# Transposing q and k on VectorE instead of TensorE in a fused attention and Fourier-mixing kernel

## Chip, cores and metric

The kernel runs on one core of a Trainium2 chip. The metric is the device time of one launch in microseconds. Lower is better; what is given is the median of ten executions. The profile is of one execution of the ten.

## What is computed

The reference is an attention with a threshold, followed by a Fourier mixing layer with a two-layer network. Cut to what matters:

```python
# q, k, v: [batch 8, heads 8, seq 576, head_dim 64] float32; tau a scalar
scores = 0.125 * q @ k.T                         # per batch and head, 576 x 576
thresh = max(scores, -1) - tau
scores = where(scores >= thresh, scores, -1e9)
attn = exp(scores - max(scores, -1));  attn /= sum(attn, -1) + 1e-9
x = (attn @ v)  -> [8, 576, 8 * 64]              # heads side by side
mixed = real(fft(fft(x, axis=1), axis=2))
u = x + mixed
out = u + relu(layernorm(u) @ w_ch1) @ w_ch2     # 512 -> 2048 -> 512
```

All of it is in float32. The change touches only the way in which q and k reach the product of the scores.

## The kernel before

**Pairs and steps.** The eight heads of a batch are worked in four pairs, so there are 32 pairs, numbered n. Head 0 of a pair lies on partitions 0 to 63, head 1 on 64 to 127. The 576 queries of a pair are worked in five steps (t = 0 to 4): four of 128 queries, in which each head has its own score tile, and one of the last 64 queries, in which both heads share one tile (head 0's queries on its upper half, head 1's on its lower). The main loops run over i = 5 n + t.

**How q and k get transposed.** The score product contracts over head_dim, so q and k are needed with head_dim on the partitions: `qT` and `kT`, 128 x 576 each for the pair. `load_pair(n)` brings both heads' rows into one tile `qk` (nine blocks of 128 rows by 2 x 64 values, one buffer) with ten transfers. `prep_pair(n)`, or its generator `prep_in_parts(n)`, turns the nine blocks on TensorE, through three PSUM banks: `pq` (four blocks of q, L398), `pk` (four of k, L405) and `pt` (the last 64 rows of both, L409). VectorE empties `pq` into `qT` and multiplies by the scale on the way (L399), ScalarE empties `pk` into `kT` (L406), and VectorE empties the two halves of `pt` (L410, L413). Then the transfers of pair n + 1 are issued.

In `kT`, head 1's keys stand with its last 64 first, because of where the transfers put them; the later transposition of the weights relies on that order.

**Scores.** `scores(i)` multiplies, for t < 4, 64 rows of `qT` with halves of 288 keys of `kT`, one product per head and half (L433); the two heads' products use the two row halves of the array. For t = 4 there are five products of 64 x 64 weights (L444), head 1's cut into three because of the order of its keys. Each product in float32 is two instructions of TensorE.

**After the scores.** `softmax(i)` takes the maxima on VectorE (L461), the exponentials on ScalarE (L469), the threshold (L473), and the comparison with the sum on VectorE (L477). The score tiles (`sc`, two buffers, four PSUM banks) are free after that. One step later `weights_in_parts` transposes the weights on TensorE (`pe` L541 and L544, `pw` L560), ScalarE copies them out, and after steps 2 and 0 `weighted_values` multiplies them with v (L589). The four remaining PSUM banks (`mm`) are shared by everything else.

**The order of work.** In the first batch (`step`, pairs 0 to 3) and the second (`second_batch`, pairs 4 to 7) the program's order is each engine's order. During the first batch the weights are also read, converted (L288 to L320) and centred, and TensorE is kept busy with idle products (`busy`, L112). From the third batch on (the last loop, pairs 8 to 31) the program's order is kept for TensorE alone; the other engines' and the transfers' orders come from a planner. There `fill()` puts the mixing and the network of the earlier batches (L822, L848, L926, L1090) between the pieces of the attention, so many products to each step. When the attention is through, the rest of the network is worked off.

Before, the preparation of the next pair stands at the end of step 4 in the first batch, at step 3 of the second, and in three parts over step 3 in the last loop.

Of the kernel before, what the change touches and what calls it, by code (L numbers as in the profile page):

```python
# [47 lines left out]
def kernel(  # L48
# [75 lines left out]
    def load_pair(n, queue=nc.sync):  # L124
        b, p = n // NPAIR, PAIRS[n % NPAIR]
        hs = [2 * p + (j + p) % 2 for j in range(2)]

        qk = sb.tile([128, 9, 2, D], FP32, tag="qk", bufs=1, name="qk_in")
        for j, h in enumerate(hs):
            nc.sync.dma_start(  # L130
                out=qk[:, 0:4, j, :], in_=q[b, h, 0:512, :].rearrange("(t p) d -> p t d", p=128)
            )
            nc.sync.dma_start(out=qk[0:64, 8, j, :], in_=q[b, h, 512:576, :])


        h = hs[0]
        queue.dma_start(
            out=qk[:, 4:8, 0, :], in_=k[b, h, 0:512, :].rearrange("(t p) d -> p t d", p=128)
        )
        queue.dma_start(out=qk[64:128, 8, 0, :], in_=k[b, h, 512:576, :])  # L140
        h = hs[1]
        queue.dma_start(out=qk[0:64, 4, 1, :], in_=k[b, h, 512:576, :])
        rows = k[b, h, 0:512, :].rearrange("(t r p) d -> p r t d", r=2, p=64)
        queue.dma_start(out=qk[64:128, 4:8, 1, :], in_=rows[:, 0])
        queue.dma_start(out=qk[0:64, 5:8, 1, :], in_=rows[:, 1, 0:3])
        queue.dma_start(out=qk[64:128, 8, 1, :], in_=rows[:, 1, 3])
        loaded[n] = qk

    def load_v(n):

# [20 lines left out]
    for u in range(2):  # L171
        for j in range(2):
            nc.gpsimd.memset(v_in[u][64 - 64 * j : 128 - 64 * j, 8 + j, :], 0.0)
    eps = const.tile([128, 1], FP32, name="eps")
    nc.vector.memset(eps[:], 1e-6)

# [205 lines left out]
    xs = {}  # L382
    sums = {}

    def prep_pair(n):
        for _ in prep_in_parts(n):
            pass

    def prep_in_parts(n):


        qk = loaded.pop(n)
        qT = sb.tile([128, S], FP32, tag="qT", name="qT")
        kT = sb.tile([128, S], FP32, tag="kT", name="kT")

        pq = ps.tile([128, 512], FP32, tag="mm", bufs=4, name="pq")
        for t in range(4):
            nc.tensor.transpose(pq[:, 128 * t : 128 * t + 128], qk[:, t, :, :], ident[:, :])  # L398
        nc.vector.tensor_scalar(  # L399
            out=qT[:, 0:512], in0=pq[:, :], scalar1=q_scale[:, :], scalar2=None, op0=ALU.mult  # L400
        )
        yield
        pk = ps.tile([128, 512], FP32, tag="mm", bufs=4, name="pk")
        for t in range(4):
            nc.tensor.transpose(pk[:, 128 * t : 128 * t + 128], qk[:, 4 + t, :, :], ident[:, :])  # L405
        nc.scalar.copy(kT[:, 0:512], pk[:, :])  # L406
        yield
        pt = ps.tile([128, 512], FP32, tag="mm", bufs=4, name="pt")
        nc.tensor.transpose(pt[:, 0:128], qk[:, 8, :, :], ident[:, :])  # L409
        nc.vector.tensor_scalar(  # L410
            out=qT[:, 512:S], in0=pt[:, 0:64], scalar1=q_scale[:, :], scalar2=None, op0=ALU.mult
        )
        nc.vector.tensor_copy(kT[:, 512:S], pt[:, 64:128])  # L413
        heads[n] = (qT, kT, v_in[n % 2])
        if n + 1 < B * NPAIR:
            load_pair(n + 1)

    def normalized(n):

# [3 lines left out]
    def scores(i):  # L423
        n, t = divmod(i, NT)
        qT, kT = heads[n][0:2]

        nh = 2 if t < 4 else 1
        sc = [ps.tile([128, 2, 512], FP32, tag="sc", name=f"sc{j}") for j in range(nh)]
        if t < 4:
            for c in range(2):  # L430
                for j in range(2):
                    hp = slice(64 * j, 64 * j + 64)
                    nc.tensor.matmul(  # L433
                        sc[j][:, c, 0:HALF], qT[hp, 128 * t : 128 * t + 128],
                        kT[hp, HALF * c : HALF * (c + 1)], start=True, stop=True,
                    )
        else:

            for j, c, c0, k0, w in (
                (0, 0, 0, 0, HALF), (1, 0, 0, 64, HALF), (0, 1, 0, HALF, HALF),  # L440
                (1, 1, 0, 64 + HALF, 512 - HALF), (1, 1, 512 - HALF, 0, 64),
            ):
                hp = slice(64 * j, 64 * j + 64)
                nc.tensor.matmul(  # L444
                    sc[0][hp, c, c0 : c0 + w], qT[hp, 512:S], kT[hp, k0 : k0 + w],
                    start=True, stop=True, skip_group_check=True,
                )
        steps[i] = (sc, nh)

# [735 lines left out]
    def step(i):  # L1185

        n, t = divmod(i, NT)
        scores(i)

        def last_stages():  # L1190
            run = chunks.pop(i - 1, None)
            for _ in range(2 if run else 0):
                next(run, None)

        if t == 1 and n > 0:
            softmax(i, lambda: weighted_values(n - 1, 1), last_stages)
            load_v(n + 1)
        elif t == 3:
            softmax(i, lambda: weighted_values(n, 0), last_stages)
        else:  # L1200
            softmax(i, None, last_stages)
        if t == 1 and n > 0:
            pass
        elif later and later[0][0] <= i:
            later.pop(0)[1](i)
        else:
            busy(2 if i < NCHUNK else 1)
        if t == NT - 1:
            prep_pair(n + 1)
        if i in chunks:  # L1210
            next(chunks[i])
        if i > 0:
            transposed_weights(i - 1)
        if i in chunks:
            next(chunks[i])
        while after and after[0][0] <= i:
            after.pop(0)[1]()
        if i > 0 and i + 3 < NCHUNK:
            chunks[i + 3] = w1_chunk(i + 3)
        if t == 2 and n > 0:  # L1220
            folds.append(fold_rows(n - 1))
        if folds and next(folds[0], True):
            folds.pop(0)
# [27 lines left out]
    raw = load_dim()  # L1251
    load_seq()
    chunks[1] = w1_chunk(1)
    prep_pair(0)
    load_v(0)
    chunks[2] = w1_chunk(2)
# [59 lines left out]
    def second_batch(i):  # L1316

        nonlocal budget
        n, t = divmod(i, NT)
        first = i - per_batch  # L1320
        if first != 1:
            scores(i)
        if first == 0:

            transposed_weights(i - 1)
        softmax(i, None, lambda: (advance(first - 1), advance(first - 1)))
        chunks.pop(first - 1, None)
        transfers(first)
        fold_more()
        if first == 0:  # L1330
            weighted_values(n - 1, 1)
            scores(i + 1)
            column_means(LAST)
            copy_mean(LAST)
            folds.append(fold_rows(n - 1))
            while folds:
                fold_more()
            load_v(n + 1)
            start_batch(0)
            mix(3)  # L1340
            mix(3)
        elif first == 1:
            mix(3)
            transposed_weights(i - 1)
            mix(2)
            mirrored(LAST)
            for c, eng in ((1, nc.vector), (3, nc.vector), (0, nc.gpsimd), (2, nc.gpsimd)):
                less_mean(eng, LAST, c)
            advance(first)
            advance(first)  # L1350
        elif first == 2:
            mix(2)
            transposed_weights(i - 1)
            mix(2)
            weighted_values(n, 0)
            advance(first)
            advance(first)
        else:
            fill()
            transposed_weights(i - 1)  # L1360
            advance(first)
            advance(first)
            fill()
            if t == 3:
                prep_pair(n + 1)
            fill()
            if t == 2:
                weighted_values(n, 0)
            if t == 0:
                weighted_values(n - 1, 1)  # L1370
                folds.append(fold_rows(n - 1))
                load_v(n + 1)
        if first == 16:
            fold_halves(1)
        if first < 3:
            budget += 3 * per_slot
# [10 lines left out]
    for i in range(2 * per_batch, total + 1):  # L1387
# [4 lines left out]
        n, t = divmod(i, NT)  # L1392
        if t > 2:
            fold_more()
        nothing = iter(())
        prep = prep_in_parts(n + 1) if t == 3 and n + 1 < B * NPAIR else nothing
        weights = weights_in_parts(i - 1)
        next(prep, None)
        fill()
        next(weights, None)  # L1400
        fill()
        next(weights, None)
        next(prep, None)
        if i < total:
            softmax(i)
        fill()
        next(prep, None)
        if t == 2:
            weighted_values(n, 0)
        if t == 0:  # L1410
# [60 lines left out]
```

## Time and profile before

| what | value |
|---|---|
| median of 10 runs | 1669.63 us (1667.75 to 1671.06) |
| the profiled execution's own time | 1667.75 us |
| its span, first to last instruction | 1665.9 us |
| granted TensorE clock | 0.998 |
| packets of q1, the queue of SP's transfers | 128854, 55.35 MB, 12.3% of 16 engines |
| q transfers: 64 of 128 KB and 64 of 16 KB | 2.3 and 2.2 us to landing |
| k transfers on SP: 31 of 128, 31 of 64, 31 of 48 and 93 of 16 KB | 2.1 to 2.4 us to landing |

How to read it: the span is the time from the first instruction to the last as the profiler saw them; what lies around it (1.85 us here) belongs to the time too. PE is TensorE's matmul row, PEld its weight loads, DVE VectorE, ACT ScalarE, POOL GpSimd, SP the engine that issues most transfers. A PE that is busy all the time need not be at its peak, since matmuls are pipelined and their ends are modelled. In the groups of instructions, a row gives line, engine, operation, what is written and read, shapes and count, then busy time and the mean of one in ns, then the idle time of the engine just before and who ended it.

### The profile page before, as it was taken

Reading aid. Unit: us, or ns where it says so; the run is one execution under the profiler, and the core shown is the slowest. Engines: PE = TensorE matmul, PEld = TensorE weight load, DVE = VectorE, ACT = ScalarE, POOL = GpSimd, SP = SyncE. Lnnn points to the kernel's source line nnn. Section 1 sums busy time; section 2 is a strip of 40 time slices with the busy share of each in tenths; the row PEclk is TensorE's granted clock in tenths of the full one; section 3 lists DMA queues with packets and bytes.
Section 4 is the critical chain, followed back from the end, with each engine's and each line's share of the span. In section 5 each row is a group of like instructions: output and inputs, shape, how many; then the busy total and the mean of one; then the engine's idle time right before and its main releaser. Section 6 shows DMA issues by size and latency. Waiting matters only on the chain.

```text
span 1665.9 us, 28885 instructions
## 1 busy us (share of the span) xinstructions
PE 1616.9 (97%) x10826; PEld 1271.8 (76%) x10826; DVE 1146.1 (69%) x2518; ACT 838.0 (50%) x1817; POOL 583.5 (35%) x779
## 2 busy tenths in 40 slices
PE   8998999999999999999999999999999999999998
PEld 4555555577887778878888788887878787889998
DVE  6887785567757686857575868686777768664454
ACT  5765775444455454545354546454646455532111
POOL 5774562042311452133331143214242244115232
PEclk9999999999999999999999999999999999999999
DMA  5423221100010001010001010101001010000000
GB/s 165 114 55 110 73 87 43 34 15 22 22 35 19 24 15 42 23 28 14 23 22 35 15 28 15 43 22 29 22 17 41 22 32 4 14 1 13 14 13 13
DMA packets 130384, 57.48 MB, mean 35 GB/s; under 512 B 121123, under 2 KB 121125, under 8 KB 130246
## 3 DMA queue, kind: packets, MB, share of 16 engines
q1 hardware_dynamic: 128854, 55.35, 12.3%
q8 instruction: 86, 1.41, 0.3%
q14 instruction: 52, 0.43, 0.1%
q10 hardware_dynamic: 1392, 0.30, 0.1%
HBM read 46.02 MB, written 9.44 MB: 33 GB/s over the span
## 4 chain that ended last, share of the span: by engine, by line
PE 75%; DVE 14%; ACT 7%; issue 2%; POOL 1%; DMA 0%; SPq 0%; DVEq 0%; ACTq 0%; POOLq 0%
PE ph L926 23%; PE po L1090 18%; PE pv L589 8%; PE sc L433 7%; PE pw L560 5%; PE po L848 3%; DVE e L477 3%; DVE neg L461 2%; ACT e L469 2%; DVE hs L1051 2%; PE sc L444 2%; PE ph L822 1%; PE py L692 1%; PE pa L709 1%; PE pn L782 1%
## 5 line engine op out<-in xcount | busy, mean ns | idle before, releaser
L469 ACT ACTIVATE e<-sc,neg 128x576 f32<-128x576 f32 x288 | 212.5, 738 | 236.3 <-DVE neg L461 235.6
L461 DVE TENSOR_REDUCE neg<-sc 128x1 f32<-128x576 f32 x288 | 206.2, 751 | 170.9 <-PE sc L433 158.7
L477 DVE SCALAR_TENSOR_TENSOR e<-sc,thr,e 128x576 f32<-128x576 f32 x288 | 229.8, 811 | 57.5 <-ACT thr L473 54.1
L1090 PE MATMUL po<-w,hs 128*128 128x256 f32 x1024 | 246.3, 383 | 0.5 <-DVE u L804 0.5
L1090 PEld LDWEIGHTS po<-w,hs 128*128 128x128 f32 x1024 | 186.0, 190 | 33.6 <-issue 11.2
L926 PE MATMUL ph<-u_t,w 128*128 128x128 f32 x1536 | 187.2, 276 | 0.0
L926 PEld LDWEIGHTS ph<-u_t,w 128*128 128x128 f32 x1536 | 178.7, 192 | 4.4 <-issue 3.3
L560 PE MATMUL pw<-ident,e 128*128 128x128 f32 x1152 | 169.5, 274 | 10.4 <-ACT kT L406 2.7
L562 ACT COPY e_t<-pw 128x512 f32<-128x512 f32 x256 | 148.7, 595 | 59.8 <-PE pw L560 59.1
L433 PE MATMUL sc<-kT,qT 64*128 64x288 f32 x1024 | 168.0, 429 | 7.0 <-DVE e L477 6.4
L560 PEld LDWEIGHTS pw<-ident,e 128*128 128x128 f32 x1152 | 134.2, 141 | 29.3 <-issue 4.3
L935 DVE TENSOR_TENSOR hs<-ph,hs 128x512 f32<-128x512 f32 x160 | 107.0, 685 | 71.3 <-PE ph L926 46.7
L433 PEld LDWEIGHTS sc<-kT,qT 64*128 64x128 f32 x1024 | 92.9, 186 | 69.0 <-issue 37.2
L926 PE MATMUL ph<-t_u,s_w 128*128 128x128 f32 x1024 | 126.0, 276 | 2.2 <-POOL t_u L900 1.8
L804 DVE SCALAR_TENSOR_TENSOR u<-po,rstd,u 128x256 f32<-128x256 f32 (+1 forms) x164 | 75.5, 484 | 73.8 <-PE po L1090 71.9
L926 PEld LDWEIGHTS ph<-t_u,s_w 128*128 128x128 f32 x1024 | 119.4, 192 | 5.3 <-issue 2.6
L1090 PE MATMUL po<-hs,s_tile 128*128 128x256 f32 x512 | 122.0, 382 | 0.0
L496 ACT ACTIVATE e<-e,den 128x576 f32<-128x576 f32 x96 | 74.9, 780 | 67.3 <-DVE den L489 66.6
L1090 PEld LDWEIGHTS po<-hs,s_tile 128*128 128x128 f32 x512 | 93.6, 190 | 13.6 <-issue 2.1
L943 ACT ACTIVATE hs<-hs 128x512 f32<-128x512 f32 x112 | 69.3, 630 | 64.0 <-DVE hs L935 63.9
L622 POOL TENSOR_TENSOR half<-x 128x287 f32<-128x287 f32 x48 | 40.7, 869 | 126.1 <-ACT x L595 70.7
L1086 POOL TENSOR_TENSOR hs<-hs,s_tile 128x512 f32<-128x512 f32 x32 | 42.4, 1325 | 117.5 <-PE po L1090 113.8
(199 smaller groups left out, 2900.8 us busy)
## 6 DMA issues: line engine op xcount, KB each, us to landing
hs<-in_moe_w_ch_dram SPq DMA_DIRECT2D x23, 512.0 KB, 4.3
out_dram<-u SPq DMA_DIRECT2D x36, 256.0 KB, 2.2
qk_in<-in_q_dram SPq DMA_DIRECT2D x64, 128.0 KB, 2.3
v_in<-in_v_dram SPq DMA_DIRECT2D x64, 128.0 KB, 2.4
qk_in<-in_k_dram SPq DMA_DIRECT2D x31, 128.0 KB, 2.4
w<-in_moe_w_ch_dram SPq DMA_DIRECT2D x6, 512.0 KB, 7.6
qk_in<-in_k_dram SPq DMA_DIRECT2D x31, 64.0 KB, 2.3
stage<-in_moe_w_ch_dram SPq DMA_DIRECT2D x3, 512.0 KB, 3.8
```

Of the source, the lines that this page charges most:

```text
L433: nc.tensor.matmul(sc[j][:, c, 0:HALF], qT[hp, 128 * t : 128 * t + 128], kT[hp, HALF * c : HALF * (c + 1)], start=True, stop=True,)
L461: nc.vector.tensor_reduce(out=neg[:, j : j + 1], in_=sc[j][:, :, 0:HALF], axis=AXIS_XY, op=ALU.max, negate=True,)
L469: nc.scalar.activation(out=ej, in_=sc[j][:, :, 0:HALF], func=ACT.Exp, bias=neg[:, j : j + 1], scale=1.0)
L477: nc.vector.scalar_tensor_tensor(out=ej, in0=sc[j][:, :, 0:HALF], scalar=thr[:, j : j + 1], in1=ej, op0=ALU.is_ge, op1=ALU.mult, accum_out ...
L496: nc.scalar.activation(out=e[:, S : 2 * S], in_=e[:, S : 2 * S], func=ACT.Copy, scale=den[:, 1:2])
L560: nc.tensor.transpose(pw[:, c, :], e[:, c0 : c0 + 128], ident[:, :])
L562: nc.scalar.copy(e_t[:, 4 * j : 4 * j + 4, qs], pw[:, :, :])
L589: nc.tensor.matmul(pv[64 * j : 64 * j + 64, 0:m], vt[:, 2 * c + j, :], e_t[:, 4 * j + c, 0:m] if c < 4 else ends[:, 0:m], start=(c == 0), ...
L804: nc.vector.scalar_tensor_tensor(out=u, in0=product, scalar=self.rstd[:, t : t + 1], in1=u, op0=ALU.mult, op1=ALU.add,)
L926: nc.tensor.matmul(banks[name][:, 128 * q : 128 * q + 128], left[c][:, 512 * part + 128 * q : 512 * part + 128 * q + 128], right[c], start ...
L935: nc.vector.tensor_tensor(out=to, in0=bank, in1=to if other is None else other, op=ALU.add)
L1090: nc.tensor.matmul(bank[:, 0 : DM // 2], left[p], right[p], start=start and p == 0, stop=p == NK - 1, skip_group_check=True,)
```

## The change

`load_pair` now fills two tiles, `q_in` and `k_in` (128 x 576, one buffer each), with eight transfers. Each takes 32 of the 64 columns of one head, all 576 rows, and places every block of 32 rows side by side on 32 partitions, in runs of 128 bytes. VectorE then transposes each 32 x 32 block where it stands (`nc.vector.transpose`), and the result is head_dim by position.

`prep_pair` has three such transpositions: k's 576 columns, once more the last 64 keys of head 1 into the columns ahead of them (so that head 1's keys can still be read with the last 64 first; `kT` is 64 columns wider), and q's 576 columns into `qT`, which has one buffer now instead of two. TensorE's nine transpositions, the PSUM banks and the four copies out of them are gone.

The scaling of q is an operation of its own, `scale_q`: on ScalarE for pair 0, else on GpSimd, in place, at step 2 of the pair before. `prep_ends`, at step 1, copies the two heads' last 64 queries on GpSimd into a 128 x 128 tile `q_ends` that is zero elsewhere; the scores of step 4 are then two products of 128 x 128 weights with both heads' keys.

The preparation of the next pair stands at step 3 everywhere, in one piece: in the first batch and the second behind the softmax of that step, in the last loop ahead of it in the program.

```diff
 def load_pair(n, queue=nc.sync):
-        qk = sb.tile([128, 9, 2, D], FP32, tag="qk", bufs=1, name="qk_in")
...
+        raws = []
+        for src, name, eng in ((q, "q_in", nc.sync), (k, "k_in", queue)):
+            raw = sb.tile([128, S], FP32, tag=name, bufs=1, name=name)
+            for j, h in enumerate(hs):
+                for g in range(2):
+                    p = 64 * j + 32 * g
+                    eng.dma_start(
+                        out=raw[p : p + 32, :].rearrange("p (r d) -> p r d", d=32),
+                        in_=src[b, h, :, 32 * g : 32 * g + 32].rearrange(
+                            "(r p) d -> p r d", p=32
+                        ),
+                    )
+            raws.append(raw)
+        loaded[n] = raws
...
+    q_ends = const.tile([128, 128], FP32, name="q_ends")
+    nc.gpsimd.memset(q_ends[:, :], 0.0)
...
+    def scale_q(n):
+        raw = loaded[n][0]
+        if n == 0:
+            nc.scalar.activation(out=raw[:, :], in_=raw[:, :], func=ACT.Copy, scale=q_scale[:, :])
+        else:
+            nc.gpsimd.tensor_scalar(
+                out=raw[:, :], in0=raw[:, :], scalar1=q_scale[:, :], scalar2=None, op0=ALU.mult
+            )
...
 def prep_pair(n):
...
+        q_raw, k_raw = loaded.pop(n)
+        kT = sb.tile([128, D + S], FP32, tag="kT", name="kT")
+        nc.vector.transpose(kT[:, D : D + S], k_raw[:, :])
+        nc.vector.transpose(kT[64:128, 0:D], k_raw[64:128, 512:S])
+        qT = sb.tile([128, S], FP32, tag="qT", bufs=1, name="qT")
+        nc.vector.transpose(qT[:, :], q_raw[:, :])
...
+    def prep_ends(n):
+        for j in range(2):
+            hp = slice(64 * j, 64 * j + 64)
+            nc.gpsimd.tensor_copy(q_ends[hp, hp], heads[n][0][hp, 512:S])
...
 def scores(i):
...
-                    hp = slice(64 * j, 64 * j + 64)
+                    hp, k0 = slice(64 * j, 64 * j + 64), D * (1 - j)
...
-                        kT[hp, HALF * c : HALF * (c + 1)], start=True, stop=True,
+                        kT[hp, k0 + HALF * c : k0 + HALF * (c + 1)], start=True, stop=True,
...
-            for j, c, c0, k0, w in (
-                (0, 0, 0, 0, HALF), (1, 0, 0, 64, HALF), (0, 1, 0, HALF, HALF),
-                (1, 1, 0, 64 + HALF, 512 - HALF), (1, 1, 512 - HALF, 0, 64),
-            ):
-                hp = slice(64 * j, 64 * j + 64)
+            for c in range(2):
                 nc.tensor.matmul(
-                    sc[0][hp, c, c0 : c0 + w], qT[hp, 512:S], kT[hp, k0 : k0 + w],
-                    start=True, stop=True, skip_group_check=True,
+                    sc[0][:, c, 0:HALF], q_ends[:, :], kT[:, D + HALF * c : D + HALF * (c + 1)],
+                    start=True, stop=True,
                 )
...
-        if t == NT - 1:
+        if t == 2:
+            scale_q(n + 1)
+        if t == 3:
             prep_pair(n + 1)
+        if t == 1:
+            prep_ends(n)
```

The last lines are of the first batch (`step`); the second batch and the last loop get the same three calls. At the start, `scale_q(0)` stands ahead of `prep_pair(0)`.

More of the change, by code (lines that the diff above doesn't have):

```diff
@@ L126, in load_pair @@
         hs = [2 * p + (j + p) % 2 for j in range(2)]
-        qk = sb.tile([128, 9, 2, D], FP32, tag="qk", bufs=1, name="qk_in")
[L129 to L147, printed above, removed]
+        raws = []
[12 more added lines that the diff above has]
+        loaded[n] = raws
     def load_v(n):
@@ L383 @@
     sums = {}
-    def prep_pair(n):
[L386 to L413, printed above, removed]
+    def scale_q(n):
[6 more added lines that the diff above has]
+            )
+    def prep_pair(n):
+        q_raw, k_raw = loaded.pop(n)
[4 more added lines that the diff above has]
+        nc.vector.transpose(qT[:, :], q_raw[:, :])
         heads[n] = (qT, kT, v_in[n % 2])
@@ L1253 @@
     chunks[1] = w1_chunk(1)
+    scale_q(0)
     prep_pair(0)
@@ L1372, in second_batch @@
                 load_v(n + 1)
+        if t == 1:
+            prep_ends(n)
+        if t == 2:
+            scale_q(n + 1)
         if first == 16:
@@ L1394 @@
             fold_more()
-        nothing = iter(())
-        prep = prep_in_parts(n + 1) if t == 3 and n + 1 < B * NPAIR else nothing
         weights = weights_in_parts(i - 1)
-        next(prep, None)
+        if t == 1:
+            prep_ends(n)
+        if t == 2 and n + 1 < B * NPAIR:
+            scale_q(n + 1)
+        if t == 3 and n + 1 < B * NPAIR:
+            prep_pair(n + 1)
         fill()
@@ L1402 @@
         next(weights, None)
-        next(prep, None)
         if i < total:
@@ L1406 @@
         fill()
-        next(prep, None)
         if t == 2:
```

## The prediction

> **What bounds the kernel now.** I read the page from the top: busy time by engine, then the slices, then the same by stage (the windows view), and last the order of instructions around one preparation of a pair.
>
> ```profile
> PE 1616.9 (97%) x10826; PEld 1271.8 (76%) x10826; DVE 1146.1 (69%) x2518; ACT 838.0 (50%) x1817; POOL 583.5 (35%) x779
> ...
> PE   8998999999999999999999999999999999999998
> PEld 4555555577887778878888788887878787889998
> DVE  6887785567757686857575868686777768664454
> ```
>
> PE is full nearly everywhere, but PEld is not: in slices 1 to 6 weight loads are at 5 tenths while VectorE is at 7 to 8. There the PE row is filled by `busy` (L112), which computes nothing. The windows (after the two times: PE, PEld, DVE, ACT, POOL busy, clock, DMA share, GB/s) split the kernel:
>
> ```profile
> 66.00:105.00 39.00, 36.22 (x199) 21.30 (x197) 33.94 (x76) 30.62 (x71) 30.32 (x32) 1.00 0.34 92
> ...
> 282.00:1480.00 1198.00, 1181.22 (x8243) 952.74 (x8242) 835.45 (x1858) 617.31 (x1317) 354.92 (x473) 1.00 0.09 24
> ```
>
> In the first batch VectorE is busy 33.9 of 39 us, in a loop scores, maximum, exponent, threshold. From 282 us, where the third batch begins, to 1480 us TensorE is idle 1198.0 - 1181.2 = 16.8 us for 24 pairs, 49 us each (some 9.8 us for each of five steps). There a microsecond taken off TensorE is nearly a microsecond of the kernel, if nobody else falls behind. TensorE's timeline of one pair in that stage shows what the change touches (start, duration, instruction, idle before it):
>
> ```profile
> 1036.99 1.24 PE L433 MATMUL sc<-kT,qT 64*128 64x288 f32 x8
> 1038.16 0.66 PE L398 MATMUL pq<-ident,qk_in 128*128 128x128 f32 x4
> 1038.78 1.99 PE L1090 MATMUL po<-w,hs 128*128 128x256 f32 x8
> ...
> 1041.37 0.66 PE L560 MATMUL pw<-ident,e 128*128 128x128 f32 x4 [0.48 <-DVE qT L399]
> ...
> 1044.03 0.60 PE L405 MATMUL pk<-ident,qk_in 128*128 128x128 f32 x4
> 1044.47 2.76 PE L1090 MATMUL po<-hs,s_tile 128*128 128x256 f32 x12
> 1047.06 0.27 PE L409 MATMUL pt<-ident,qk_in 128*128 128x128 f32 x1
> 1047.26 1.20 PE L444 MATMUL sc<-kT,qT 64*64 64x288 f32 x10
> 1048.39 0.92 PE L1090 MATMUL po<-hs,s_tile 128*128 128x256 f32 x3
> ```
>
> Durations overlap, so I read start to next start: pq 0.62, pk 0.44, pt 0.20, the last 64 queries' scores 1.13 us. Once, pw waited 0.48 us because the pq bank was still being emptied by VectorE.
>
> **What the skill says.** "VectorE: DVE Perf Modes", The three transpose paths: VectorE transposes 32x32 blocks only, into SBUF; so the blocks must be placed by the transfer, as the diff does. No row of this trace is such a transposition. "Vector Engine (DVE) Microarchitecture Reference", The reshape front-end: the transposition sustains one element per cycle per lane. "SBUF — State Buffer", SBUF: two separate sides: VectorE and GpSimd exclude each other on a shared port pair; the trace agrees, `e<-e,den` (L492) takes 0.52 us alone and 1.54 us at 1035.80, beside a 1.93 us GpSimd operation. "DMA: Bandwidth & Descriptors", Why small descriptors are slow: at 256 bytes and below each packet's fixed cost tells; here q1's 128854 packets took 12.3% of 16 x 1665.9 us, 25.4 ns each at 430 bytes on average.
>
> **TensorE, 24 late pairs.** 23 preparations lose nine transpositions. By the gaps above they are 0.62 + 0.44 + 0.20 = 1.26 us; at the steady pace (pk: four in 0.44) 9 x 0.11 = 0.99. I take 1.1: 25.3 us. The last scores go from ten instructions on quarters of the array, two running side by side, to four full ones (two products, two passes each). Eight 256-column instructions follow each other at 0.216 us in the chain of waits (1.73 us), so 288 columns are 0.243 and four are 0.97: a gain of only 1.13 - 0.97 = 0.16 us, 24 times, 3.8 us. The waits of pw on qT, 1.9 us in this stage, go too. Sum 31.0 us.
>
> **VectorE.** Three evictions go, two transpositions of 576 and one of 64 columns come.
>
> ```profile
> L399 DVE TENSOR_SCALAR qT<-pq,q_scale 128x512 f32<-128x512 f32 x32 | 23.7, 739 | 5.3 <-PE pq L398 5.3
> L410 DVE TENSOR_SCALAR qT<-pt,q_scale 128x64 f32<-128x64 f32 x32 | 8.8, 276 | 6.8 <-PE pt L409 6.8
> L413 DVE COPY kT<-pt 128x64 f32<-128x64 f32 x32 | 6.8, 213 | 0.0
> ```
>
> Removed: 0.74 + 0.28 + 0.21 = 1.23 us a pair. Added: by the Perf Modes page (58 cycles + one per element at 0.96 GHz) 0.66 us for 576 columns, an estimate; the bounds are L492's 0.52 and two cycles per element, about 1.3 us. I take 0.68 twice and 0.15, 1.51 us: net +0.3 a pair, from 0 to +1.6. Late in the kernel VectorE has 1198 - 835 = 363 us to spare, 15 us a pair, which hides it on average. But all 1.5 us now stand in one place, ahead of the maxima of step 3 (t = 3), and the qT transposition waits there for that step's scores, since qT has one buffer. Queued behind it: maximum, threshold, then TensorE's next scores, which need the `sc` buffers. At 1036.99 VectorE was itself 1.1 us late with the maxima, and freed `sc` at 1042.7, 4.5 us ahead of the next scores. 1.5 us fits. I give back 4 us for the pairs where it doesn't.
>
> **ScalarE, GpSimd, queues.** ScalarE loses kT's copy, 0.60 us a pair; off the path late. GpSimd gains the scaling of q (128x576, between its copy of 630 columns at 0.71 and a two-operand 512 at 1.28; taken 0.9 us) and two 64x64 copies (the 32-column copy is 0.24: 0.25 each): 1.4 us a pair on 30% busy in this stage; hidden, but by the shared port part of it lengthens VectorE's operations (in the 4 us). SP issues 8 transfers a pair for 10, at some 0.58 us each: 1.2 us less in front of v, swaps and stores. Packets double, 2304 to 4608, halved in size: at most 4608 x 25.4 ns / 16 = 7.3 us a pair, against 4 steps (39 us late, 20 us in the first batch) from the release of the buffers to `scale_q`. Hidden, except at the start. Late stage: -31 + 4 = **-27 us**.
>
> **First two batches, 8 preparations.** Here VectorE and ScalarE share the path. In batch one the pair boundary looked so:
>
> ```profile
> 67.68 0.73 DVE L399 TENSOR_SCALAR qT<-pq,q_scale 128x512 f32<-128x512 f32 x1
> ...
> 68.20 1.09 PE L560 MATMUL pw<-ident,e 128*128 128x128 f32 x8 [0.64 <-ACT kT L406]
> ...
> 69.22 1.24 PE L433 MATMUL sc<-kT,qT 64*128 64x288 f32 x8
> ...
> 70.49 1.42 DVE L461 TENSOR_REDUCE neg<-sc 128x1 f32<-128x576 f32 x2 [0.99 <-PE sc L433]
> ```
>
> Without pq, pk, pt and kT's copy the scores at 69.22 could start some 1.5 us sooner; in exchange 1.5 us of transpositions come a step earlier (t = 3 for t = 4), of which about 1.2 us delays the next maxima. Net -0.3 in batch one, -0.5 in batch two (TensorE is busy 30.6 of 34 us from 216 us): -3 us for eight, with ends -12 (all boundaries won, all transpositions in gaps) and +8.
>
> **Start.** Nothing covers the first load: 7.3 us of packets for 3.7. The path after landing (ScalarE scaling 0.74, kT, qT) is about as long as the old one, 8.4 to 10.4 us. I take +1.5, from -1 (fewer transfers on the queues) to +5.
>
> **Sum.** -27 - 3 + 1.5 = -28.5 us. The profiled execution took 1667.75 us (span 1665.9 and 1.85 around it), 1.9 below the median of 1669.63: 1639.2 in its terms, 1641 in the median's.
>
> **Rivals.** *A, VectorE at half rate (0.13):* transpositions of 1.3 us. Net +1.6 for +0.3 a pair: 8 x 1.3 = 10 us more in the first batches, and some 0.2 us a pair late, 5 us: 1656. For: VectorE runs without a gap for 13 us from 1028.4 on. Against: the page's one element per cycle.
>
> *B, slower: GpSimd's queue (0.12).* The scaling goes into a queue that runs in order and holds instructions waiting for TensorE:
>
> ```profile
> POOL s_w L909 <- PE ph L926: 167.4, 18, 14.0
> ```
>
> If `scale_q` stands behind such a wait (up to 14 us) for longer than the 9.8 us of a step, the qT transposition stops VectorE with the softmax behind it, and TensorE's scores stop next. Above 31/23 = 1.3 us a pair this eats the whole gain; at 2.2 us it is 20 us slower: 1690. For: those waits. Against: GpSimd is idle 843 of 1198 us in this stage, and what precedes the scaling in the program is mostly released by TensorE before step 3.
>
> *C, transfers (0.10):* 128-byte packets take the same 25 ns beside w1's chunks (DMA share 0.64 from 10 to 37 us), and scaling waits in batch one, 3 us a pair for 3 pairs, with +5 at the start: 1653.
>
> *D, the block-diagonal product brings nothing (inside the forecast):* +3.8 us.
>
> **Numbers.** Forecast 0.65, its own range 1629 to 1653. The range 1627 to 1662 takes in A and C; B and part of the tails stay outside. A measurement of this kernel can tell about 0.2% (3.3 us) from no change. Faster: 0.65 + 0.11 of A + 0.08 of C = 0.84; same 0.03; slower: B's 0.11 and 0.02 of C = 0.13.
>
> **What would show it.** Right: PE has 288 + 192 instructions fewer or so (9 transpositions and 6 score instructions for each of 32 pairs), the last scores 0.97 us start to next, transpositions near 0.68 us, idle TensorE from batch three on still under 25 us for 24 pairs, each pair about 1.2 us shorter. Wrong: transpositions over 1 us; "qT waits for POOL q_in" in VectorE's waits, with maxima late at t = 3; TensorE waiting for `e`, or first scores after 13 us.

## The result and the profile after

The changed kernel takes **1636.97 us** (median of 8 runs, 1635.47 to 1639.23) against 1669.58 for the kernel before (median of 29): ratio 0.9807, 95% interval 0.9798 to 0.9815. The forecast was 1641, with 1627 to 1662 as its range. The profiled execution took 1637.42 us with a span of 1635.3; before, these were 1667.75 and 1665.9.

The page of the changed kernel, busy time by engine and the slices:

```profile
PE 1586.6 (97%) x10346; PEld 1250.0 (76%) x10346; DVE 1171.9 (72%) x2518; ACT 821.5 (50%) x1786; POOL 660.0 (40%) x875
...
PE   8998899999999999999999999999999999999998
```

TensorE has the 480 instructions fewer that were forecast, and still fills 97% of a shorter span. VectorE gained 25.8 us and GpSimd 76.5, and neither sets the end. By stage, in the changed kernel (after the two times: PE, PEld, DVE, ACT, POOL busy, clock, DMA share, GB/s):

```profile
10.00:128.00 118.00, 109.15 (x530) 61.85 (x531) 103.39 (x234) 83.27 (x184) 92.19 (x134) 0.94 0.41 106
128.00:282.00 154.00, 138.50 (x722) 84.98 (x721) 124.75 (x267) 96.63 (x224) 87.89 (x109) 0.98 0.30 81
282.00:1450.00 1168.00, 1152.43 (x7897) 935.00 (x7896) 850.03 (x1860) 603.51 (x1294) 412.91 (x544) 1.00 0.12 25
```

and the first of these windows in the kernel before:

```profile
10.00:128.00 118.00, 108.53 (x588) 62.69 (x588) 99.99 (x234) 85.35 (x189) 83.14 (x122) 0.99 0.38 106
```

In the first batch TensorE is as busy as before with 58 matmul instructions fewer, at a lower clock, while VectorE and GpSimd are busier. That fits a stage which gained nothing.

**Where the 30.6 us of the two traces lie.** I take the start of each pair's last-scores product as a clock that ticks once a pair. At pair 7 it stands at 280.5 us before and 280.8 after: eight pairs, no gain. At pair 31 it stands at 1458.0 and 1428.0. So 24 pairs gained 30.4 us, 1.27 each, and what follows (208 and 207 us) is the same. The four products, pair 7 and pair 31, first of the kernel before, then of the changed one:

```profile
280.54 1.18 PE L444 MATMUL sc<-kT,qT 64*64 64x288 f32 x9
1458.03 1.18 PE L444 MATMUL sc<-kT,qT 64*64 64x288 f32 x9
...
280.84 0.89 PE L436 MATMUL sc<-kT,q_ends 128*128 128x288 f32 x3
1427.97 1.14 PE L436 MATMUL sc<-kT,q_ends 128*128 128x288 f32 x4
```

Summing start to next start by kind of instruction over those 24 pairs, the rows `pq`, `pk` and `pt` (12.94 + 10.06 + 4.66 = 27.66 us) are gone and the last scores went from 27.00 to 23.29; that is 31.4. All other rows together grew by 1.0. TensorE's idle time from 282 to 1450 us is 15.6 us after (1168.0 - 1152.4 in the window above) and 16.1 before (1168.0 - 1151.9):

```profile
282.00:1450.00 1168.00, 1151.89 (x8017) 927.90 (x8017) 816.32 (x1816) 601.21 (x1283) 349.86 (x469) 1.00 0.10 24
```

One pair's last scores in TensorE's timeline of the changed kernel:

```profile
1023.95 2.76 PE L1082 MATMUL po<-hs,s_tile 128*128 128x256 f32 x12
1026.54 1.13 PE L436 MATMUL sc<-kT,q_ends 128*128 128x288 f32 x4
1027.51 1.03 PE L1082 MATMUL po<-hs,s_tile 128*128 128x256 f32 x4
1028.37 1.03 PE L1082 MATMUL po<-w,hs 128*128 128x256 f32 x4
```

No `pt` stands ahead of the scores now, and they last 1027.51 - 1026.54 = 0.97 us, as forecast. The new operations, in the groups of the changed kernel (busy us, mean ns of one, idle before):

```profile
L404 DVE STREAM_TRANSPOSE qT<-q_in 128x576 f32<-128x576 f32 x32 | 24.7, 771 | 0.3
L402 DVE STREAM_TRANSPOSE kT<-k_in 64x64 f32<-64x64 f32 x32 | 7.8, 242 | 0.6
L390 POOL TENSOR_SCALAR q_in<-q_in,q_scale 128x576 f32<-128x576 f32 x31 | 56.8, 1832 | 18.5 <-DMA q_in<-in_q_dram 17.2
```

The idle time before the q transposition is 0.3 us in 32 pairs: the transfers and the scaling practically never made VectorE wait. The planner also broke up the block of transpositions that the prediction put ahead of the maxima of step 3. VectorE's timeline of the changed kernel shows q's alone between the two maxima:

```profile
1020.48 0.75 DVE L453 TENSOR_REDUCE neg<-sc 128x1 f32<-128x576 f32 x1
1021.14 0.76 DVE L404 STREAM_TRANSPOSE qT<-q_in 128x576 f32<-128x576 f32 x1
1021.84 0.71 DVE L453 TENSOR_REDUCE neg<-sc 128x1 f32<-128x576 f32 x1
```

This q is of pair 23; k of the same pair had been transposed at 984.3 us. For pairs 10 to 31 the planner puts k's transposition 35 to 52 us, some four steps, ahead of q's. Pair 24 shows it in two lines:

```profile
1029.38 0.76 DVE L401 STREAM_TRANSPOSE kT<-k_in 128x576 f32<-128x576 f32 x1
...
1064.64 0.77 DVE L404 STREAM_TRANSPOSE qT<-q_in 128x576 f32<-128x576 f32 x1
```

So in the late stage only q's 0.77 us is left at step 3.

### The profile page after: what moved, and what is told of

Its sections match the earlier page's. It is cut to its first block, busy times and chain, and to the rows that moved or that the text cites. A ratio compares the mean times of both kernels' runs of the same rounds, so it can differ in the third digit from the quotient of the medians.

```text
span 1635.3 us, 27989 instructions
## 1 busy us (share of the span) xinstructions
PE 1586.6 (97%) x10346; PEld 1250.0 (76%) x10346; DVE 1171.9 (72%) x2518; ACT 821.5 (50%) x1786; POOL 660.0 (40%) x875
## 3 DMA queue, kind: packets, MB, share of 16 engines
q1 hardware_dynamic: 200438, 55.34, 14.5%
## 4 chain that ended last, share of the span: by engine, by line
PE 77%; DVE 13%; ACT 5%; issue 2%; POOL 1%; DMA 1%; SPq 1%; DVEq 0%; ACTq 0%; POOLq 0%
PE ph L918 24%; PE po L1082 20%; PE pv L581 9%; PE sc L430 7%; PE pw L552 5%; PE po L840 3%; DVE e L469 2%; DVE neg L453 2%; PE ph L814 2%; ACT e L461 2%; PE sc L436 1%; PE pa L701 1%; PE py L684 1%; PE pn L774 1%; DVE hs L1043 1%
## 5 line engine op out<-in xcount | busy, mean ns | idle before, releaser
L430 PE MATMUL sc<-kT,qT 64*128 64x288 f32 x1024 | 174.3, 433 | 12.9 <-DVE e L469 11.3
L430 PEld LDWEIGHTS sc<-kT,qT 64*128 64x128 f32 x1024 | 96.2, 187 | 77.9 <-issue 39.0
```

Of the source, the lines that this page charges most:

```text
L430: nc.tensor.matmul(sc[j][:, c, 0:HALF], qT[hp, 128 * t : 128 * t + 128], kT[hp, k0 + HALF * c : k0 + HALF * (c + 1)], start=True, stop=True,)
```

## The experiments

**Theory:** from the third batch on TensorE is the bound, so each TensorE microsecond removed is a microsecond gained, and what VectorE, GpSimd and the queues took on is hidden. In the first two batches VectorE with ScalarE is the bound, and what was removed there is paid back by what was added. **Rivals:** the added VectorE work costs late as well (A, which the prediction tied to a transposition at half rate); GpSimd's scaling holds VectorE (B); the block-diagonal product brings nothing (D).

### The change in one stage alone

`e1_late_only` uses the new way for pairs 9 to 31 and the old one for pairs 0 to 8; `e2_early_only` is its reverse. Both share one pair of tiles for q and k.

```diff
+    def blocks(n):
+        return n > 2 * NPAIR          # e2: n <= 2 * NPAIR
...
 def prep_pair(n):
+        if not blocks(n):
+            for _ in prep_in_parts(n):
+                pass
+            return
```

> Pairs 9 to 31 are prepared the new way (block transpositions, scaling on GpSimd, last scores as one block-diagonal product); pairs 0 to 8 the old way, on TensorE, at their old places. Theory (the gain is TensorE's time in the stage that TensorE bounds): pairs 9 to 31 keep all of their 1.3 us, so 1667.5 - 30 = some 1637 to 1639 us, ratio 0.981 to 0.983, within 2 us of the changed kernel. Rival (the first two batches hold part of the gain, by earlier starts that the rest only carries on): well above, 1643 us or more.

> The reverse: pairs 0 to 8 the new way, pairs 9 to 31 the old way, in three parts over step 3. Theory: the first two batches gain nothing, since three transpositions of VectorE and 1.8 us of GpSimd stand there against TensorE's time that is not on the path: within 3 us of the kernel before, ratio 0.998 to 1.001. Rival: they gain the 3 us or more that were forecast for them, or the share that the late pairs don't hold: 1664 us or less, ratio 0.997 or less.

Late only: 1641.10 us, ratio 0.9833 (0.982 to 0.9846). Early only: 1667.73, ratio 0.9989 (0.9983 to 0.9996). Early only keeps about 6% of the gain, so the first two batches are worth 0.04 to 0.17%, less than the 0.2% that I took for measurable. Late only fell 2 us outside what I expected. Its trace is 2.8 us behind the changed kernel at pair 7 and 3.5 at pair 31: the late pairs keep nearly all their gain, and the loss lies mostly in its first eight pairs. There this run prepares the old way, and yet stands at 283.6 us at pair 7 where the kernel before stood at 280.5. It has one `qT` buffer and a separate tile for the last 64 queries, so this is a cost of the edit (which part of it is not separated), and the run doesn't say that the new way helps early.

### VectorE's added work, late and early

`e4_more_late` does k's large transposition three times for pairs 9 to 31, `e5_more_early` for pairs 0 to 8.

```diff
-        nc.vector.transpose(kT[:, D : D + S], k_raw[:, :])
+        for _ in range(3 if n > 2 * NPAIR else 1):     # e5: n <= 2 * NPAIR
+            nc.vector.transpose(kT[:, D : D + S], k_raw[:, :])
```

> As the changed kernel, but for pairs 9 to 31 the 576-column transposition of k is made three times over: 1.54 us more of VectorE a pair, 35 us in all, ahead of everything that stands behind it. Theory (VectorE's slack at step 3 hides its work, TensorE bounds): at most +5 us, 1637 to 1642, ratio 0.981 to 0.984. Rival (VectorE is next to being the bound): a large part of the 35 us, 1650 us or more, ratio 0.989 or more.

> As the changed kernel, but for pairs 0 to 8 the 576-column transposition of k is made three times over: 1.54 us more of VectorE a pair. Theory (in the first two batches VectorE is on the path, and its transpositions are what gave TensorE's saving back there): pair 0 in full and most of it for the other eight, +8 to +14 us, 1645 to 1651, ratio 0.986 to 0.990. Rival (they fall into VectorE's waits there too; something else holds the first two batches, GpSimd's scaling or the transfers): +1.5 to +4 us, 1641 at most, ratio 0.983 or less.

Late: 1637.48 us, ratio 0.9809 (0.9796 to 0.9823), no difference from the changed kernel. The group of the late run shows that the work was done, 46 more of them, 35.5 us:

```profile
L402 DVE STREAM_TRANSPOSE kT<-k_in 128x576 f32<-128x576 f32 x78 | 60.1, 770 | 4.3 <-DMA k_in<-in_k_dram 3.6
```

So at nearly twice its VectorE cost the late preparation would still be free, and rival A falls for that stage. In this trace too the planner sets k's transpositions 35 us or more ahead of q's from pair 10 on; the run doesn't show that all of this work in one piece at step 3 would be free. Early: 1659.35, ratio 0.9926 (0.9913 to 0.9939). The 18 more transpositions are 13.9 us and cost 22.4, more than either side expected. VectorE is on the path there; with all that came with it, each added microsecond costs 1.6.

The trace shows where part of the excess can come from. TensorE's timeline of the changed kernel in the first batch, with the idle time ahead in brackets:

```profile
39.14 1.28 PE L430 MATMUL sc<-kT,qT 64*128 64x288 f32 x6 [1.61 <-DVE e L469]
40.35 3.59 PE L112 MATMUL pd<-ones 128*128 128x512 f32 x4
43.78 0.27 PE L533 MATMUL pe<-ident,e 128*128 128x128 f32 x1
```

The four instructions of the idle products take 43.78 - 40.35 = 3.43 us, 0.86 each. One lasts 0.59 by the median of the 50, and at the steady pace of 256 columns in 0.216 us 512 columns follow in 0.43: here they run at half speed. The windows of the changed kernel around them (last three columns: clock, DMA share, GB/s):

```profile
35.00:40.00 5.00, 3.38 (x20) 2.12 (x18) 3.84 (x10) 3.50 (x9) 2.60 (x3) 1.00 0.62 100
40.00:45.00 5.00, 5.00 (x14) 2.28 (x12) 4.30 (x11) 4.56 (x12) 2.57 (x3) 0.66 0.78 229
45.00:50.00 5.00, 5.00 (x36) 2.97 (x35) 4.51 (x12) 4.23 (x10) 2.46 (x4) 1.00 0.32 105
```

After a window with TensorE busy for 3.38 of 5 us, the clock is 0.66 in the next, and full again after that: 5 x 0.34 = 1.7 us lost, as half speed for 3.4 us would give. The Trainium skill describes this in "TensorE: Matmul & The Clock Gate", Part 1: The HAM clock gate: the clock is halved after a window of about 3.4 us of too little activity, until a busy one has passed. The trace agrees on the half and on the length; it adds that a gap of 1.61 us was enough here. A gap of that size is not always followed by a drop: after one of 1.76 us that ended at 165.11 in the same trace the clock is 1.00 from 165 to 170 us, and after one of 2.53 us that ended at 224.21 in the kernel before it is 1.00 from 225 to 232. The half-clock stretches of the changed kernel's first batch begin at 16.31, 40.20, 70.92 and 108.47 us, which is 7, 9 and 11 times 3.413 us apart. They keep a fixed beat, so where in it a gap falls may decide; no run tests this. In `e5_more_early` a gap of 2.08 us that ended at 43.88 was followed by a whole 5-us window at half:

```profile
45.00:50.00 5.00, 5.00 (x10) 2.07 (x8) 4.37 (x12) 3.54 (x7) 2.34 (x3) 0.50 0.74 224
```

Over both early stages its clock is 0.90 and 0.93. By these means it lost some 12 us of TensorE clock more than the changed kernel (118 x 0.04 + 154 x 0.05 = 12.4), enough to explain the 8.5 of excess. How much of it reached the end is not separated: if all of it did, 10 of the 22.4 us are left to VectorE's 13.9. The six runs of `e5_more_early` fit a large share: from 1654.49 us at a clock of 0.987 to 1661.18 at 0.983, the time rises by 6.7 us where 6.7 us more of clock are lost. That is a correlation, since longer gaps give both. The next run tries it for the changed kernel.

### More filler against the lower clock

`e11_more_filler` adds one idle product to every step of the first batch that has any.

```diff
-            busy(2 if i < NCHUNK else 1)
+            busy(3 if i < NCHUNK else 2)
```

> The changed kernel with one more idle product (0.6 us of TensorE that computes nothing) in each step of the first batch that has any. It asks whether the lower granted clock of the first batch (0.94 from 10 to 128 us, 0.99 in the kernel before) comes from TensorE's gaps. Theory: gaps lower the clock, and filling them gives it back: 0.98 or more in that window, and 1634 to 1637.5 us, with the filler hidden in gaps. Rival: the clock is lowered by the work itself or by chance, and the filler is 0.6 us for TensorE in each of some 16 steps: clock 0.95 or less and 1640 to 1647.

1637.57 us, ratio 0.9807 (0.9794 to 0.982). Its first window:

```profile
10.00:128.00 118.00, 113.42 (x548) 64.41 (x549) 103.17 (x234) 83.73 (x184) 92.33 (x134) 0.97 0.42 107
```

The filler is 22 instructions in all, 11 products of two each. They cost no time and brought none, so neither theory nor rival held. In this profile the clock is 0.97 for 0.94, but that can be chance. `e2_early_only` and `e3_five_products` have no more filler than the changed kernel and show 0.97 in this window too:

```profile
10.00:128.00 118.00, 105.49 (x528) 60.14 (x525) 102.52 (x233) 83.30 (x183) 91.38 (x132) 0.97 0.42 106
10.00:128.00 118.00, 107.25 (x552) 60.42 (x553) 103.32 (x234) 83.10 (x184) 92.09 (x134) 0.97 0.41 106
```

Over the whole span the changed kernel's executions have clocks from 0.991 to 0.997, and this run's from 0.993 to 0.998. So whether filler gives clock back is not shown. Nor is it shown what the lower clock costs the changed kernel: of its nine executions with a recorded clock (the median above is of eight of them) those at 0.996 and 0.997 took 1635.5 to 1636.2 us, those at 0.991 to 0.994 took 1637.4 to 1639.8. So some of the early loss may be the clock's. Its share stays open there and in `e5_more_early`.

### The block-diagonal product

`e3_five_products` keeps VectorE's transposition but goes back to five products of 64 x 64 for the last scores.

```diff
-            for c in range(2):
-                nc.tensor.matmul(
-                    sc[0][:, c, 0:HALF], q_ends[:, :], kT[:, D + HALF * c : D + HALF * (c + 1)],
-                    start=True, stop=True,
-                )
+            for j, c, c0, k0, w in (
+                (0, 0, 0, D, HALF), (1, 0, 0, D, HALF), (0, 1, 0, D + HALF, HALF),
+                (1, 1, 0, D + HALF, 512 - HALF), (1, 1, 512 - HALF, 0, 64),
+            ):
+                hp = slice(64 * j, 64 * j + 64)
+                nc.tensor.matmul(
+                    sc[0][hp, c, c0 : c0 + w], q_ends[hp, 0:64], kT[hp, k0 : k0 + w],
+                    start=True, stop=True, skip_group_check=True,
+                )
```

> As the changed kernel, but the last 64 queries' scores as five products of 64 x 64 weights again (q_ends holds both heads' last queries in 64 columns, copied by GpSimd as before). Theory: only TensorE's time counts, 1.12 for 0.97 us, 24 late pairs: +3.7 us, to 5 with the first eight pairs and the change of array mode: 1640.5 to 1642 us, ratio 0.983 to 0.984. Rival (side by side the five cost no more, the full-array product is worth nothing): 1637 us, ratio 0.981.

1645.11 us, ratio 0.9854 (0.9838 to 0.9869): 8.1 us slower than the changed kernel, twice what was expected, and far from rival D. The same stretch of TensorE's timeline, in this run:

```profile
1029.54 2.75 PE L1086 MATMUL po<-hs,s_tile 128*128 128x256 f32 x12
1032.23 1.20 PE L440 MATMUL sc<-kT,q_ends 64*64 64x288 f32 x10
1033.35 1.13 PE L1086 MATMUL po<-hs,s_tile 128*128 128x256 f32 x4
1034.32 1.03 PE L1086 MATMUL po<-w,hs 128*128 128x256 f32 x4
```

The scores take 1.12 us for 0.97. But the twelve products ahead take 2.69 for 2.59, and the four behind 0.97 for 0.86: neighbours of the same shape are 0.10 and 0.11 us longer. Together 0.36 us a pair; over the 24 late pairs this trace falls behind by 8.0 us, 0.33 a pair, of which the scores' own rows are 3.7 and the other rows 4.3, 0.18 a pair. The Trainium skill's "TensorEngine Tiling (Array Packing)", Key Properties, says that a change of tiling mode drains TensorE. This run fits that, and prices a change from the full array to quarters and back at 0.18 us on average, 0.21 in the pair shown.

### Scaling q elsewhere, and the place of the preparation

`e6_scale_on_act` scales q on ScalarE for all pairs, `e9_act_early` for pairs 0 to 8 only. `e7_scale_at_3` issues GpSimd's scaling directly ahead of the transpositions instead of one step earlier.

```diff
 def scale_q(n):
-        if n == 0:
+        if True:                      # e9: if n <= 2 * NPAIR
             nc.scalar.activation(out=raw[:, :], ...
...
# e7, in all three loops
-        if t == 2:
-            scale_q(n + 1)
         if t == 3:
+            scale_q(n + 1)
             prep_pair(n + 1)
```

> As the changed kernel, but q is scaled on ScalarE for every pair (0.77 us there instead of 1.83 us of GpSimd, which was busy 92 of 118 us in the first batch). Theory (VectorE holds the first two batches): within 2 us of the changed kernel, ratio 0.980 to 0.982, with some loss where ScalarE is on the path. Rival (GpSimd holds them): 3 us or more faster, 1634 or less, ratio 0.979 or less. From the third batch on neither expects a difference, TensorE being the bound.

> The changed kernel with q scaled by ScalarE for pairs 0 to 8 and by GpSimd for the rest. It places the 4.3 us that ScalarE's scaling brought when it was used for all pairs. Theory: a GpSimd operation of 1.8 us delays q's transposition and lengthens VectorE's operations in the first two batches, where VectorE is on the path; later it is hidden. Then about 2 us of the 4.3 (what the trace showed at pair 7) come back here and the rest, late, does not: 1634 to 1636 us. Rival: all 4.3 us come from the first batches, the late part being the planner's order for the same work: 1631 to 1633.5. Second rival: the late part alone counts: 1636 to 1638.

> As the changed kernel, but scale_q stands at step 3, directly ahead of the transpositions, so that q's transposition waits for GpSimd's queue and 1.8 us of scaling behind at most 1.0 us of k's transpositions. This puts the price of the rival of GpSimd's queue to the test. Theory: 1 to 2 us a pair in the first two batches, where the order is the program's, +7 to +14 us; in the last loop VectorE's other work is put in between or the slack takes it, +3 us at most: 1644 to 1653, ratio 0.985 to 0.990. Rival (also in the last loop the softmax behind the wait holds TensorE): 1 us or more for each of 23 pairs on top, 1665 or more.

ScalarE for all: **1632.67 us**, ratio 0.9776 (0.9764 to 0.9789), 4.3 us better than the changed kernel, and its interval lies clear of the changed kernel's. The theory's 2 us failed, and the number is the one that the rival gave. One scaling there takes 0.78 us for GpSimd's 1.83. ScalarE early only: 1635.31, ratio 0.9793 (0.978 to 0.9807). Its trace is 1.9 us ahead at pair 7 and exactly 1.9 at pair 31, so this trace has its whole gain in the first two batches, as its theory had it. By the medians it is 1.7 us, and its interval overlaps the changed kernel's, so the size is not clear of noise. The rest of `e6_scale_on_act`, about 2 us that neither side expected, comes at pairs 24 and 28, the first pairs of the last two batches; no wait of TensorE names it, and it stays open.

Scaling at step 3: 1640.59, ratio 0.9829 (0.9816 to 0.9841), less than both sides expected. Its profiled execution was longer than its median (span 1642.7); in that trace it is 8.4 us behind at pair 4 and 7.4 at the end, so all of it is early. VectorE's waits in this run hold the row

```profile
DVE qT L404 <- POOL q_in L390: 6.8, 7, 1.3
```

(us in total, times, longest): seven waits, about one for each preparation of the first two batches. None comes later: where rival B expected the scaling to stop VectorE, even this order costs nothing.

`e8_prep_at_4` puts the first batch's preparation back at step 4; `e10_k_ahead` takes `e6_scale_on_act` and puts k's transpositions at step 2 in the first two batches.

```diff
 def step(i):
...
-        if t == 3:
+        if t == NT - 1:               # e8
             prep_pair(n + 1)
# e10: in step and second_batch
         if t == 2:
             scale_q(n + 1)
+            prep_k(n + 1)
```

> As the changed kernel, but in the first batch (4 preparations) the transpositions stand at step 4, as the old ones did, ahead of the next pair's first scores. Theory: there 1.8 us of VectorE stand directly between the step's threshold and the next maxima, partly beside TensorE's transposition of the weights and the next scores: +0.5 to +1.5 us a pair, 1639 to 1643, ratio 0.982 to 0.984. Rival (the forecast's own term: at step 3 they cost 1.2 us of delay, so the place is no better): 1637 or less.

> ScalarE scales q for all pairs, and in the first two batches k's two transpositions (1.0 us) stand one step ahead of q's, at step 2; from the third batch on nothing is moved. Theory: in the first two batches the preparation holds the next step's maxima for as long as it takes in one piece, and less when it is cut in two and each piece falls beside an exponential: 2 to 6 us under the 1632.7 of ScalarE's scaling alone, 1627 to 1631. Rival one: VectorE's total sets the pace there and the place of the pieces does not: 1631.5 to 1634. Rival two: k's transfers have not landed by step 2 in batch one and VectorE waits for them: 1635 or more, with waits of VectorE on k_in in the trace.

At step 4: 1644.95, ratio 0.9851 (0.9838 to 0.9864), 8 us slower, more than expected. TensorE's waits from 10 to 282 us in this run:

```profile
PE sc L430 <- DVE qT L404: 12.7, 6, 3.0
```

Over the same stretch this wait is 1.6 us in all in the changed kernel: at step 4 the three transpositions stand directly ahead of the next pair's first scores, in the place where the old evictions stood. Step 3 is the better place by far. Dividing the preparation over two steps brings 1632.02, ratio 0.9769 (0.9756 to 0.9782): the same as `e6_scale_on_act` within the intervals, which is the number of its first rival. That VectorE's total sets the pace there is not shown by it: `e8_prep_at_4` has the changed kernel's total and is 8 us slower than it.

## Why the prediction held, step by step

**TensorE late, right.** The forecast took 31.0 us off TensorE and got 31.4. The transpositions were worth 27.66 and not 25.3, which is 1.20 us for each of 23 preparations: the gaps read before (1.26) were nearly the right price, and the lower steady pace that I averaged in was not. The 1.9 us of pw waits went, but TensorE's idle time fell by 0.5 only, and other short waits made up the rest. So the sum came out as close as it did in part by luck: one term was 2.4 too small and another some 1.4 too large.

**The last scores, right in the row and too small as a whole.** The row itself gained 3.7 us, forecast 3.8. The run with five products puts the edit's worth at 8.1, because the neighbours pay too. That isn't 4 us more of gain in the sum, since all other rows of the two kernels together differ by 1.0 only. In the kernel before, `pt` stood ahead of the scores, and part of that price may lie in its 0.20 us.

**The give-back of 4 us, too large.** The other TensorE rows grew by 1.0. I had put all three transpositions ahead of the maxima of step 3; the planner put k's some four steps earlier, and nearly doubling the work was free. So the late stage gave -30.4 for the forecast -27.

**Durations.** VectorE's transposition took 0.77 us, forecast 0.68 (0.52 to 1.3). The estimate of 0.66 from "VectorE: DVE Perf Modes" is 14% low. The page itself warns that 58 cycles are too few and gives about 150 as measured, for a copy; with that the same estimate is 0.76. One element per cycle is the right reading: from 64 columns (0.242 us) to 576 (0.771) each column takes 1.03 ns, where half rate would take twice that by the page's clock. GpSimd's scaling took 1.83 on average for my 0.9: the nearest row, a copy, was the wrong neighbour. By the traces that mistake cost about 2 us early; whether it cost any late stays open (the 2 us of `e6_scale_on_act`). Packets cost 18.9 ns each for the 25.4 forecast (14.5% of 16 x 1635.3 us over 200438), and a quarter of a tile landed in 2.3 us, so rival C had no ground.

**First two batches, the term that failed.** Forecast -3, measured +0.6 in the traces: +0.3 at pair 7, which holds a gain of 0.3 at the start. I let the removed waits count at 1.5 us and the transpositions at 1.2. VectorE added 1.78 us for 1.23 removed. GpSimd's scaling is worth 1.9 us over eight pairs by one trace. Added VectorE work costs 1.6 times its length here by the early run, the lower clock included. The clock itself (0.991 to 0.997 over the changed kernel's executions, 0.997 to 1.000 over those of the kernel before) was no term of the prediction, and its share is not separated. The prediction was also wrong that `busy` fills the PE row in this stage: before, its instructions take 19.2 of the 108.5 us that PE is busy from 10 to 128 us.

**Start, wrong in sign.** Forecast +1.5, measured -0.3: in the changed kernel the first scores start at 10.09 us for 10.40.

```profile
10.09 1.24 PE L430 MATMUL sc<-kT,qT 64*128 64x288 f32 x8 [0.88 <-DVE qT L404]
```

The last of k's transfers has been issued at 3.95 us for 5.80 before, and packets were cheaper than taken.

The errors partly cancel, which is luck: -3.4 late, +3.6 in the first batches, -1.8 at the start and -0.2 in what lies behind pair 31 and around the span make the 1.8 us between the 1639.2 forecast for the profiled execution and its 1637.42.

## What to carry to other kernels

Move work off the engine that bounds the stage and price its cover by stage: the same added transpositions were free where VectorE had 15 us a pair to spare and a planner to place them, and cost 1.6 times their length, lower clock included, where it was busy 103 of 118 us. When an operation moves to another engine, price it from a row of that engine and that kind; GpSimd's multiplication took two and a half times as long as the copy by which I had priced it. Ask of a small product in another array shape what its neighbours lose, not only what it takes itself.

## What the runs showed of the hardware that was not expected

- A change from full-array products to 64 x 64 ones and back lengthened the neighbours by 0.10 and 0.11 us in the pair shown, 0.18 together on average.
- GpSimd multiplied 128 x 576 float32 values by a per-partition factor in 1.83 us on average, where ScalarE took 0.78.
- TensorE's clock fell to half for about 3.4 us after gaps of 1.61 and 2.08 us in the first batch, and stayed full after others of 1.76 and 2.53 us. The half-clock stretches began whole multiples of 3.413 us apart.
- Eleven more idle products in the first batch cost no time. That they raised the clock is not shown.
